# Batch 0 by whole-array products, v loaded in place, 96-row blocks, loads tied to the turns of q, part of FFN1's activation off PSUM, and the lists of the order anew

## The chip, the cores and the metric

The kernel runs on one core of one Trainium2 chip. The metric is the device time of one execution, in microseconds, as the median of the runs. Its engines each work through a queue of their own, in the order of the program: TensorE (PE) for products, VectorE (DVE), ScalarE (ACT), GpSimd (POOL), and SyncE (SP), which here only issues DMAs. GpSimd issues the loads from HBM, SyncE the DMA transposes and the stores.

## The reference

Four batches of eight heads, 768 tokens and 64 values a head, in 8 blocks of 96 tokens. A learned 8 × 8 matrix per head mixes the blocks of k and of v ("sorting"), each block of q then attends to its own sorted block, and the result goes through a two-layer network with a leaky activation.

```python
P = sort_net                                     # (4, 8, 8, 8)
for _ in range(5):                               # Sinkhorn
    P = exp(P - max(P, -1)); P = P / (sum(P, -1) + 1e-9); P = P / (sum(P, -2) + 1e-9)
k_sorted = einsum('bhij,bhjcd->bhicd', P, k_blocks)
v_sorted = einsum('bhij,bhjcd->bhicd', P, v_blocks)
scores = q_blocks @ k_sorted.T / sqrt(64)        # 96 x 96 per block and head
attn = softmax(scores); x = (attn @ v_sorted)    # -> (3072, 512), heads side by side
h = x @ w_in                                     # (512, 2048)
g = max(h, 0) + alpha * min(h, 0)
out = g @ w_out                                  # (2048, 512), float32
```

## The kernel before, in words

The work is written as operations in a graph, each with an engine (or a choice of two), a duration for the planner, the keys of what it reads and writes, and a priority. A table of numbers (`SEQ`) gives the order of all operations; a letter behind a number picks the engine where there is a choice. `arrange` lays them out by that table, and `emit` puts each engine's operations into its queue in that order, with semaphore waits only where a key asks for one. So each engine's order is fixed, and an operation that waits holds everything behind it on its engine.

The 32 blocks (four batches of eight, `g` counts them) go through `attention`, in three kinds. All of batch 0 is "near": its scores are taken, the maximum over each row found on VectorE, the scores taken again transposed and the maximum subtracted by further products (`s2`), and ScalarE's exponential gives the transposed weights directly. The later batches are "far": scores once, maximum, eight exponentials per block on ScalarE, and a DMA transpose by SyncE (`Esb` to `ET`). Then for all the output product with v, which carries a column of ones for the sum, a reciprocal and a product on VectorE (`xq`), and the transpose of `xq` into `xT`: by four products and a copy for batches 0 and 1, by a DMA transpose for batches 2 and 3.

Sorting is a product too: `prep_k` and `prep_v` multiply k or v with a small block matrix made from P (`BDK` for batch 0, `BDM` and `BDV` for the others). For the later batches k and v are first copied by GpSimd or another engine into tiles with zeros between the heads (`conv_k` into `KSz`, `conv_v` into `VDz`), so that one product uses the whole array; for batch 0, products on half the array do without for k, and v is copied into a zeroed piece of `hT`. The sorted blocks take 112 rows, 16 of them padding. q of batch 0 is loaded whole and turned by products (`prep_q`), the later batches' q is loaded per head into `QN` and turned by six DMA transposes (`turn_q`, into `QTz`).

The network runs over chunks of 2, 2, 4, 4, ... blocks. One FFN1 step (`ffn1`) is four products for 128 of the 2048 hidden columns, 192 or 384 tokens wide, into one PSUM bank; ScalarE's `Relu(-h)` and VectorE's multiply-add read that bank and write `hT`. One tile of FFN2 (`ffn2`) is 128 tokens, 16 products in four parts, all into one bank until the last part is done; most tiles use the same bank, `psY`.

All loads stand in GpSimd's queue: q, k, v of batch 0, k of batch 1, w_in in four pieces of 128 rows each, w_out in two halves, then the rest. Every FFN1 step reads all four pieces of w_in. `fill` and `idle` put products without use (`warm`, line 865) into gaps that the planner expects on TensorE up to 130 us, and a burst of 110 tiny products (line 945) starts it.

## Time and profile before

| | |
|---|---|
| median of 3 runs (lowest, highest) | 242.4 us (242.17, 244.28) |
| span of the profiled execution, first to last instruction | 240.3 us |
| TensorE busy | 231.3 us (96%), 2490 products |
| VectorE, ScalarE, GpSimd busy | 171.3, 154.1, 100.0 us |
| granted TensorE clock, mean | 1.000 |
| chain of waits: share of TensorE | 85% |

The profiled execution's own time is known by its span alone; the median of the runs lies 2.1 us above it. In the rows below, L and a number is the line of the kernel, "out<-in" names the tiles, and a time in brackets behind a row is how long the engine stood idle before it, and for whom. A product's length in a row counts until its result is written; products follow one another closer than that, so a group's length in the chain of waits, which counts from one group to the next, is its price.

### The profile page before, as it was taken

Reading aid. Unit: us, or ns where it says so; the run is one execution under the profiler, and the core shown is the slowest. Engines: PE = TensorE matmul, PEld = TensorE weight load, DVE = VectorE, ACT = ScalarE, POOL = GpSimd, SP = SyncE. Lnnn points to the kernel's source line nnn. Section 1 sums busy time; section 2 is a strip of 40 time slices with the busy share of each in tenths; the row PEclk is TensorE's granted clock in tenths of the full one; section 3 lists DMA queues with packets and bytes.
Section 4 is the critical chain, followed back from the end, with each engine's and each line's share of the span. In section 5 each row is a group of like instructions: output and inputs, shape, how many; then the busy total and the mean of one; then the engine's idle time right before and its main releaser. Section 6 shows DMA issues by size and latency. Waiting matters only on the chain.

```text
span 240.3 us, 6202 instructions
## 1 busy us (share of the span) xinstructions
PE 231.3 (96%) x2490; PEld 143.0 (59%) x2519; DVE 171.3 (71%) x347; ACT 154.1 (64%) x423; POOL 100.0 (42%) x146
## 2 busy tenths in 40 slices
...
GB/s 100 209 214 213 187 213 192 173 208 174 177 44 145 166 92 172 160 175 169 139 115 65 117 137 76 112 174 71 138 126 112 120 52 172 43 0 44 0 91 131
DMA packets 71981, 31.36 MB, mean 130 GB/s; under 512 B 64512, under 2 KB 67344, under 8 KB 71952
## 3 DMA queue, kind: packets, MB, share of 16 engines
...
q8 instruction: 20, 0.33, 0.5%
...
HBM read 27.28 MB, written 6.29 MB: 140 GB/s over the span
## 4 chain that ended last, share of the span: by engine, by line
PE 85%; POOL 5%; DMA 4%; DVE 2%; issue 1%; ACT 1%; POOLq 0%
PE psH L880 33%; PE psYP L919 29%; DMA VST<-in_v_dram 4%; PE psS L919 4%; PE psS L769 3%; PE psO L825 3%; PE psYP L726 2%; PE psYP L685 2%; POOL QN L457 2%; PE psS L784 1%; PE psYP L865 1%; POOL VDz L428 1%; PE psO L851 1%; PE psO L731 1%; PE psS L793 1%
## 5 line engine op out<-in xcount | busy, mean ns | idle before, releaser
L893 DVE SCALAR_TENSOR_TENSOR hT<-t,omaT,psH 128x384 bf16<-128x384 f32 (+1 forms) x139 | 77.8, 571 | 29.6 <-ACT t L890 27.6
L880 PE MATMUL psH<-xT,w_in_bf 128*128 128x384 bf16 (+1 forms) x556 | 98.4, 311 | 0.2 <-DVE hT L893 0.2
L890 ACT ACTIVATE t<-psH 128x384 f32<-128x384 f32 (+1 forms) x139 | 62.6, 461 | 49.8 <-PE psH L880 48.6
L919 PE MATMUL psYP<-w_out_bf,hT 128*128 128x512 bf16 x309 | 77.8, 379 | 1.7 <-DVE outstg L428 0.2
L880 PEld LDWEIGHTS psH<-xT,w_in_bf 128*128 128x128 bf16 x556 | 48.9, 98 | 28.9 <-DVE hT L893 4.1
L919 PEld LDWEIGHTS psYP<-w_out_bf,hT 128*128 128x128 bf16 x336 | 31.2, 98 | 30.3 <-DVE outstg L428 0.6
L805 ACT ACTIVATE Esb<-psS,nf 96x96 bf16<-96x96 f32 x192 | 46.2, 345 | 2.0 <-DVE nf L778 1.8
L428 POOL COPY VDz<-VST 64x384 bf16<-64x384 bf16 x40 | 34.1, 852 | 20.0 <-PE psYP L726 12.5
L672 POOL COPY KSz<-KS 64x512 bf16<-64x512 bf16 x36 | 22.6, 628 | 13.8 <-PE psYP L685 9.7
L778 DVE TENSOR_REDUCE nf<-psS 96x8 f32<-96x768 f32 x24 | 22.8, 948 | 5.5 <-PE psS L769 5.1
L836 DVE TENSOR_TENSOR xq<-psO,rec 96x512 bf16<-96x512 f32 x31 | 21.2, 684 | 0.6
L457 POOL DMA_DIRECT2D QN<-in_q_dram x24 | 19.8, 835 | 0.3 <-POOL QN L517 0.3
L865 PE MATMUL psYP<-identb 128*128 128x512 bf16 x45 | 14.8, 457 | 0.7 <-ACT identb L428 0.7
L825 PEld LDWEIGHTS psO<-VS,ET 112*128 112x128 bf16 x248 | 11.3, 98 | 4.3 <-ACT ET L816 0.2
L769 PEld LDWEIGHTS psS<-KT,QTz 128*96 128x96 bf16 x192 | 11.8, 125 | 2.5
L825 PE MATMUL psO<-VS,ET 112*128 112x65 bf16 x248 | 12.7, 194 | 0.1
L833 DVE RECIPROCAL rec<-psO 96x8 f32<-96x8 f32 x31 | 6.2, 201 | 9.1 <-PE psO L825 9.0
L428 ACT ACTIVATE VS<-psYP 112x512 bf16<-112x512 f32 x15 | 10.3, 688 | 3.6 <-PE psYP L726 3.0
L769 PE MATMUL psS<-KT,QTz 128*96 128x96 bf16 x192 | 12.6, 208 | 0.0
L428 ACT ACTIVATE KT<-psYP 128x512 bf16<-128x512 f32 x15 | 8.9, 596 | 3.9 <-PE psYP L685 2.5
L726 PE MATMUL psYP<-BDV,VDz 128*128 128x64 bf16 x192 | 9.6, 193 | 1.0 <-POOL VDz L428 0.9
L726 PEld LDWEIGHTS psYP<-BDV,VDz 128*128 128x128 bf16 x192 | 8.1, 98 | 3.9 <-POOL VDz L428 1.0
...
## 6 DMA issues: line engine op xcount, KB each, us to landing
...
KS<-in_k_dram POOLq DMA_DIRECT2D x3, 768.0 KB, 11.2
...
w_in_bf<-in_moe_w_in_dram POOLq DMA_DIRECT2D x4, 512.0 KB, 14.8
w_out_bf<-in_moe_w_out_dram POOLq DMA_DIRECT2D x2, 1024.0 KB, 22.9
...
```

The source lines that it names most:

```text
L428: return e.activation(o, i, ACTF.Copy) if e is nc.scalar else e.tensor_copy(o, i)
L457: G.add(POOL, lambda e, h=h: e.dma_start(AP(QN, h * 128 + (h // 4) * 64, [[6144, 128], [1024, 6], [1, 64]]), AP(q.tensor, b * HB + h * S * ...
L672: G.add(POOL, lambda e, hp=hp: e.tensor_copy(AP(KSz, hp * 64 * 3072 + u % 3 * 1024 + hp * 64, [[3072, 64], [128, 8], [1, 64]]), AP(KS[n], ...
L726: inst = e.matmul(AP(t, off + dd * 64, [[row, 128], [1, 64]]), AP(VDz, (u % VSL * 8 + dd) * 128, [[VSL * 1024, 128], [1, 128]]), AP(BDV, b ...
L769: inst = e.matmul(o, AP(QTz[n], hp * 3072 + h4 * 768 + i * 96, [[6144, 128], [1, 96]]), AP(KT[n], (h4 * 8 + i) * bk, [[ld, 128], [64, 2], ...
L778: G.add(DVE, lambda e: e.tensor_reduce(AP(nx, 0, [[8, 96], [4, 2], [1, 4]]), AP(psX, 0, [[1024, 96], [512, 2], [96, 4], [1, 96]]), AxisLis ...
L805: inst = e.activation(AP(Esb[me], p * 128, [[1024, 96], [64, 2], [1, 48]]), AP(psX, (p // 4) * 512 + (p % 4) * 96, [[1024, 96], [48, 2], [ ...
L825: inst = e.matmul(AP(psZ, hp * 512 + h4 * 68, [[1024, 128], [1, 65]]), AP(ET[me] if far else ET[m], pos(h4, hp) * 96, [[800, nk], [1, 128] ...
L880: inst = e.matmul(AP(pt, poff, [[1024, 128], [1, n]]), AP(w_in_bf, kt * DFF + ft * 128, [[KT_TILES * DFF, 128], [1, 128]]), AP(xT, kt * XR ...
L890: G.add(ACT, lambda e: e.activation(AP(t1[tb], 0, [[384, 128], [1, n]]), AP(pt, poff, [[1024, 128], [1, n]]), ACTF.Relu, scale=-1.0), t_ac ...
L893: G.add(DVE, lambda e: e.scalar_tensor_tensor(out=AP(hT, ft * RING + tok % RING, [[FT_TILES * RING, 128], [1, n]]), in0=AP(t1[tb], 0, [[38 ...
L919: inst = e.matmul(AP(bank[0], bank[1], [[1024, 128], [1, n]]), AP(hT, ft * RING + tok % RING, [[FT_TILES * RING, 128], [1, 128]]), AP(w_ou ...
```

## The change

- **Batch 0's sort.** k is copied into zero-spaced tiles (`KSz` and three of the `outstg` buffers) like the other batches, and sorted by whole-array products. v is loaded straight into a piece of `QTz[1]` that has been zeroed around it, in two halves, so that it needs no copy; its products take 96 columns at a stride of 64. `BDK` is gone, `spread0` makes `BDM` and `BDV` of batch 0. q of batch 0 comes in two halves by token and is turned by 48 products.
- **96-row blocks.** The padding of `KT` and `VS` to 112 rows falls away, with the copies and constants for it.
- **32-bit copies.** `conv_k` and `conv_v` move pairs of bf16 as one 32-bit element and may run on GpSimd or VectorE; the clearing of tiles may run on three engines, reading the zero tile `bz` where ScalarE does it.
- **Loads.** w_in comes in four pieces of 512 columns, each with all rows, and an FFN1 step waits for its own piece alone; w_out comes in four quarters. k and v of batch 2 are read only when all six turns of batch 1's q have landed.
- **Batch 1** turns `xq` by DMA (`TURN = 1`) instead of products.
- **FFN1's activation.** In the chunks of two blocks, five of each 16 steps (`POOLED`) have ScalarE copy the bank into `hc`, and GpSimd or VectorE forms `h - (1 - alpha) min(h, 0)` from there in two steps. The first chunk uses two banks where it used three.
- **The lists.** `SEQ` and the planner's issue times are new, so the order changes on every engine.

On GpSimd, after the first loads, before the change: w_in, then w_out's first half and v of batch 1 (`VST`), then the copies for batch 0's v (`hT`) and the first head of q (`QN`).

```order
L964 DMA w_in_bf<-in_moe_w_in_dram 128x2048
L530 MEMSET Esb 96x16x16 x2
L509 MEMSET KSz 128x1536
L964 DMA w_in_bf<-in_moe_w_in_dram 128x2048 x3
L969 DMA w_out_bf<-in_moe_w_out_dram 128x8x512
L517 MEMSET QN 128x6x64
L491 DMA VST<-in_v_dram 64x3072 x2
L428 COPY hT<-VST 128x8x48
L698 COPY KT<-KT 128x32x16
L672 COPY KSz<-KS 64x8x64
L457 DMA QN<-in_q_dram 128x6x64
```

At the same place now:

```order
L518 MEMSET QTz 64x1536
L995 DMA w_in_bf<-in_moe_w_in_dram 128x4x512 x2
L555 MEMSET Esb 96x8x16
L995 DMA w_in_bf<-in_moe_w_in_dram 128x4x512
L467 DMA QN<-in_q_dram 128x6x64
L695 COPY KSz<-KS 64x8x32 x2
L1000 DMA w_out_bf<-in_moe_w_out_dram 128x4x512
L467 DMA QN<-in_q_dram 128x6x64
L995 DMA w_in_bf<-in_moe_w_in_dram 128x4x512
L506 DMA VST<-in_v_dram 64x3072
L1010 TENSOR_SCALAR nomT<-omaT 128x16
L910 TENSOR_SCALAR t<-hc,nomT 128x192
```

The head loads of q and w_out's first quarter now stand ahead of w_in's last quarter, which follows the copies of k and a clearing of `QTz`, and v of batch 1 comes behind it; the steps of FFN1's activation (`t<-hc`) stand between the loads.

On TensorE around the first FFN1 step, with what each waits for (`d_` is a load: `wi` w_in, `wo` w_out; `s_` another engine), before:

```order
L851 MATMUL psYP<-identb,xq 128x96 x4
L851 MATMUL psO<-identb,xq 128x96 [waits s_dve]
L851 MATMUL psO<-identb,xq 128x96 x3
L613 MATMUL psYP<-Pb,selk 128x64 [waits s_act]
L613 MATMUL psYP<-Pb,selk 128x64 x2
L616 MATMUL psYP<-Pb,selk 64x64 x6
L865 MATMUL psH<-identb 128x512 x4
L880 MATMUL psH<-xT,w_in_bf 128x192 [waits d_wi0,d_wi3,d_wi2,d_wi1,s_act]
L880 MATMUL psH<-xT,w_in_bf 128x192 x3
```

and now:

```order
L864 MATMUL psO<-identb,xq 128x96 [waits s_dve]
L864 MATMUL psO<-identb,xq 128x96 x3
L878 MATMUL psH<-identb 128x512 x4
L878 MATMUL psYP<-identb 128x512
L785 MATMUL psS<-KT,QTz 96x96 [waits s_act]
L785 MATMUL psS<-KT,QTz 96x96 x7
L893 MATMUL psH<-xT,w_in_bf 128x192 [waits d_wi0,s_dve]
L893 MATMUL psH<-xT,w_in_bf 128x192 x3
L640 MATMUL psYP<-Pb,selk 128x64 [waits s_act]
L640 MATMUL psYP<-Pb,selk 128x64 x2
L643 MATMUL psYP<-Pb,selk 64x64 x6
L893 MATMUL psH<-xT,w_in_bf 128x192 x4
```

The first step waits for one piece of w_in where it waited for four.

On TensorE where the first tile of FFN2 meets w_out, before (its third part waits for the second half):

```order
L772 MATMUL psS<-KT,QTz 96x96 [waits s_act]
L772 MATMUL psS<-KT,QTz 96x96 x7
L919 MATMUL psYP<-w_out_bf,hT 128x512 [waits d_wo1]
L919 MATMUL psYP<-w_out_bf,hT 128x512 x3
L851 MATMUL psO<-identb,xq 128x96 [waits s_dve]
L851 MATMUL psO<-identb,xq 128x96 x3
```

and now, where the tile's second to fourth parts wait for a quarter each and the first score of batch 1 for the first turn of q (`d_qt0`):

```order
L945 MATMUL psYP<-w_out_bf,hT 128x512 [waits d_wo1]
L945 MATMUL psYP<-w_out_bf,hT 128x512 x3
L864 MATMUL psO<-identb,xq 128x96 [waits s_dve]
L864 MATMUL psO<-identb,xq 128x96 x3
L782 MATMUL psS<-KT,QTz 96x96 [waits d_qt0,s_act]
L782 MATMUL psS<-KT,QTz 96x96 x7
L893 MATMUL psH<-xT,w_in_bf 128x192 [waits s_dve]
L893 MATMUL psH<-xT,w_in_bf 128x192 x3
L741 MATMUL psYP<-BDV,VDz 128x64 [waits s_pool,s_act]
L741 MATMUL psYP<-BDV,VDz 128x64 x7
L893 MATMUL psH<-xT,w_in_bf 128x192 x4
L945 MATMUL psYP<-w_out_bf,hT 128x512 [waits d_wo2]
```

Behind these rows the product that waits for w_out's last quarter (`d_wo3`) comes ten rows later. Elsewhere: on VectorE the clearing of `bz`, which stood first, now follows the first Sinkhorn iteration; on SyncE `xT`'s transposes stand between `ET`'s from batch 1 on.

```diff
-BK0 = BLK + 16
...
+PHASES = [(0, 8)]
+CHUNKS = [(0, 2), (2, 4), (4, 8)]
+FAR0 = 8
+TURN = 1
+POOLED = (1, 4, 7, 10, 13)
...
 SEQ = """
-0 2 11 3 7 4 8 1 22 9 14 42 28 43 44 19 45 46 5 47 18 48 49 15 50 51 39 52 53 6 54 55 56 25 57 58 138 29 59 60
...
+27 0 5 23 22 9 13 10 36 42 43 29 44 30 11 45 46 47 48 49 50 51 41 2 1 3 14a 52 53 54 55 56 57 58 59 60 61 12a 37 39 4
...
+    def load_q0(x, prio):
+        G.add(POOL, lambda e: e.dma_start(AP(VST[0], x * 1536, [[3072, 128], [192, 8], [1, 192]]),
+                                          AP(q.tensor, x * 384 * D, [[192, 128], [S * D, 8], [1, 192]])),
+              1929, w=[("QS", x)], prio=prio, dma=(d_q[x], 0))
...
-                load_us / n, r=paced(g, x) * (b == 3), w=[(name, b % 2), (name, b % 2, x)] if x == 0 else [(name, b % 2, x)],
-                prio=prio, dma=(sem[b + x], 0))
+                load_us / n, r=paced(g, x) * (b == 3) + [("QTzt", 1, t) for t in range(6)] * (b == 2) + [("turned", 7)] * (b == 1 and FAR0 < 8), w=[(name, b % 2), (name, b % 2, x)] if x == 0 else [(name, b % 2, x)],
+                prio=prio, dma=(sem[{0: 0, 1: 1, 2: 2, 3: 6}[b] + x], 0))
...
     def load_v(b, prio):
         if b == 0:
-            load_kv(VST, v, "VST", d_v, 9, b, prio)
+            for th in range(2):
+                G.add(POOL, lambda e, th=th: e.dma_start(
+                    AP(QTz[1], th * 64 * 6144 + th * 3072, [[6144, 64], [1, 3072]]),
+                    AP(v.tensor, th * 3072, [[6144, 64], [1, 3072]])), load_us / 2,
+                    w=[("VST0", th)], prio=prio, dma=(d_v[th], 0))
             return
...
                 AP(v.tensor, b * HB + th * 3072 + c, [[6144, 64], [1, t]])), load_us / (2 * n),
-                r=[("QTzt", 0, 5)] * (b == 3), w=[("VST", b % 2)] * (x == 0) + [("VST", b % 2, x)],
-                prio=prio, dma=(d_v[2 * b - 1 + x], 0))
...
+        def f(e):
+            return copy(e, o, i) if e is nc.scalar else e.memset(o, 0.0)
+        G.add(ZERO, f, {"pool": 50 + 0.9 * n, "dve": 70 + 0.83 * n, "act": 170 + n / 1.2}, r=["bz"] + list(r), w=w, prio=prio)
...
-            for j in range(8):
-                inst = e.matmul(psYP[:, 1, 0:8], AP(sel0, j * 128, [[1024, 32], [1, 128]]),
-                                AP(Pb, j, [[64, 32], [8, 8]]), start=(j == 0), stop=(j == 7))
+            for x in range(2):
+                for j in range(8):
+                    inst = e.matmul(psYP[:, 1, x * 8:x * 8 + 8], AP(sel0, (x * 8 + j) * 128, [[2048, 32], [1, 128]]),
+                                    AP(Pb, j, [[64, 32], [8, 8]]), start=(j == 0), stop=(j == 7))
             return inst
-        G.add(PE, f, 300, r=["Pb", "sel0"], w=PSP, prio=prio)
...
+    def kslot(b, u):
+        return (outstg[u - 3], 512, 0, ("KO", u)) if b == 0 and u > 2 else (KSz, 1536, u % 3 * 512, ("KSz", u % 3))
 
     def conv_k(b, u, prio):
         n = b % 2
+        t, ld, off, key = kslot(b, u)
+        tw = KSzw if t is KSz else t
         for hp in range(2):
-            G.add(POOL, lambda e, hp=hp: e.tensor_copy(
-                AP(KSz, hp * 64 * 3072 + u % 3 * 1024 + hp * 64, [[3072, 64], [128, 8], [1, 64]]),
-                AP(KS[n], hp * 64 * 3072 + 8 * u * 64, [[3072, 64], [64, 8], [1, 64]])), 900,
-                r=[("KS", n)] + [("KS", n, x) for x in range(4)], w=[("KSz", u % 3, hp)], prio=prio)
-
...
+                kt, ld, ko, _ = kslot(b, c // 8)
+                kb = KSz if kt is KSz else outb[c // 8 - 3]
+                inst = e.matmul(AP(t, off + (c - c0) * 8 * ni, [[row, 128], [1, 8 * ni]]),
+                                AP(kb, 2 * ko + c % 8 * 128, [[2 * ld, 128], [1, 128]]),
+                                AP(BDM, b * 64 + 8 * i0, [[256, 128], [1, 8 * ni]]))
...
+            G.add(SHIFT, lambda e, o2=o2, i2=i2: e.tensor_copy(o2, i2),
+                  {"dve": 340, "pool": 519}, r=vst, w=[("VDz", u % VSL, th)], prio=prio)
...
+    def prep_v(b, d0, nd, i0, ni, prio, bank=BANK_P):
         t, off, row, keys = bank
-        n = b % 2
+        n, u = b % 2, d0 // 8
 
         def f(e):
             inst = None
-            for dd in range(8):
-                if b:
-                    inst = e.matmul(AP(t, off + dd * 64, [[row, 128], [1, 64]]),
-                                    AP(VDz, (u % VSL * 8 + dd) * 128, [[VSL * 1024, 128], [1, 128]]),
-                                    AP(BDV, b * 64, [[256, 128], [1, 64]]))
-                    continue
-                for th in range(2):
-                    inst = e.matmul(AP(t, th * 64 * row + off + dd * 64, [[row, 64], [1, 64]]),
-                                    AP(hT, (8 * u + dd) * 64, [[HR, 128], [1, 64]]),
-                                    AP(BDK, th, [[512, 128], [2, 64]]))
+            for d in range(d0, d0 + nd):
+                dd = d % 8
+                inst = e.matmul(AP(t, off + (d - d0) * 8 * ni, [[row, 128 if b else 96], [1, 8 * ni]]),
+                                AP(VDz, (u % VSL * 4 + dd // 2) * 256 + dd % 2, [[VSL * 1024, 128], [2, 128]]) if b else
+                                AP(QTz[1], d, [[6144, 128], [64, 96]]),
+                                AP(BDV, b * 64 + 8 * i0, [[256, 128], [1, 8 * ni]]))
...
-        far, me = b > 0, g % NE
-        nk = 112
+        far, me = g >= FAR0, g % NE
+        nk = 96
         pos = (lambda h4, hp: 2 * h4 + hp) if far else (lambda h4, hp: 4 * hp + h4)
...
-        if far and not (b == 1):
+        if far and b >= TURN:
             G.add(SYNC, lambda e: e.dma_start_transpose(o2, AP(xq[me], 0, [[512, 96], [1, 512]])),
                   4400 if g < 18 else 2600, r=[("xq", me)], w=[("xT", g % 16), ("turnx", g)], prio=prio, dma=(d_x[me], 0))
...
-        banks = BANK_H + ([BANK_P] if ga < 2 else [])
+        banks = BANK_H
...
-        op = G.add(PE, f, t_pe(*[(n, 128)] * 4), r=[("xT", g % 16) for g in range(ga, gb)] + [("w_in", kt) for kt in range(KT_TILES)],
+        op = G.add(PE, f, t_pe(*[(n, 128)] * 4), r=[("xT", g % 16) for g in range(ga, gb)] + [("w_in", ft // 4)],
...
+        if n == 192 and ft % 16 in POOLED:
+            y = step[0] % 2
+            h1 = AP(hc[y], 0, [[192, 128], [1, n]])
+            tt = AP(t1[tb], 0, [[384, 128], [1, n]])
+            G.add(ACT, lambda e: copy(e, h1, AP(pt, poff, [[1024, 128], [1, n]])), t_act(n), r=keys, w=[("hc", y)], prio=prio)
+            G.add(SHIFT, lambda e: e.tensor_scalar(out=tt, in0=h1, scalar1=0.0, scalar2=AP(nomT, ft, [[16, 128], [1, 1]]),
+                                                   op0=AluOpType.min, op1=AluOpType.mult),
+                  {"pool": 320, "dve": 260}, r=[("hc", y), "nomT"], w=[("t1", tb)], prio=prio)
+            G.add(SHIFT, lambda e: e.tensor_tensor(out=ho, in0=h1, in1=tt, op=AluOpType.add),
+                  {"pool": 620, "dve": 360}, r=[("hc", y), ("t1", tb)], w=hw, prio=prio)
+            return
         G.add(ACT, lambda e: e.activation(AP(t1[tb], 0, [[384, 128], [1, n]]),
...
-    load_q(0, -98)
+    load_q0(0, -98)
     load_k(0, -97)
     load_v(0, -96)
+    load_q0(1, -95.9)
     ident_op = consts()
     late_masks()
     sinkhorn()
     spread0(-48)
+    for y in range(2):
+        prep_q(0, y, -50)
     for u in range(6):
-        prep_q(u, -50, (BANK_H + BANK_O + BANK_S)[u])
-    for u in range(6):
-        prep_k(0, u, -47, BANKS0[(u + 1) % 5])
-    for u in range(8):
...
+            AP(w_in_bf, p * 512, [[KT_TILES * DFF, 128], [DFF, KT_TILES], [1, 512]]),
+            AP(moe_w_in.tensor, p * 512, [[DFF, 128], [128 * DFF, KT_TILES], [1, 512]])),
...
+            AP(w_out_bf, p * 4 * DM, [[FT_TILES * DM, 128], [DM, 4], [1, DM]]),
+            AP(moe_w_out.tensor, p * 4 * 128 * DM, [[DM, 128], [128 * DM, 4], [1, DM]])),
+            2650, w=[("w_out", p)], prio=-30 + p, dma=(dma_sem("wo%d" % p), 0))
...
-        if i == 0 and b + 1 < B:
-            if b == 0:
-                load_k(1, -26)
-            if b < 2:
-                load_q(b + 1, 8 * b - 20)
-            if b == 0:
-                load_v(1, -25)
+        if g == 8:
+            load_q(2, -12)
+        if g == 2:
+            for y in range(2):
+                prep_q(1, y, 0.9)
+            for z in PHASES[1:]:
+                phase(*z, 1, 1.5, BANK_S + BANK_O, BANK_O + [BANK_P])
         attention(g, g * 0.85 if g < 8 else g)
         if g == 1:
             spread([1, 2, 3], 1)
             G.add(PE, lambda e: warm(e, 4, (psH, 0)), 300, r=["identb"], w=[("psH", 0, 0), ("psH", 0, 1)], prio=1)
         if b + 1 < B:
-            for t in range(6 if b == 0 and i == 1 else 0):
-                turn_q(1, t, 2 + t / 2)
+            if g == 7:
+                load_k(1, -26)
```

398 lines of the change are left out of this document (200 added, 198 removed).

## The prediction

> **What bounds the kernel now.** I read the busy time by stage first, cut at the first FFN1 product (30.17), the first score product of batch 1 (58.41), 92 us and the last product (237.66). Columns: stretch, length, then busy time of each engine.
>
> ```profile
> 0.00:30.17 30.17, 26.89 (x577) 15.27 (x577) 19.24 (x66) 16.72 (x33) 24.61 (x44) 1.00 0.95 184
> 30.17:58.41 28.24, 27.74 (x424) 22.19 (x428) 24.62 (x57) 19.84 (x48) 14.96 (x22) 1.00 1.39 192
> 58.41:92.00 33.59, 32.35 (x356) 20.71 (x359) 29.49 (x56) 27.17 (x83) 26.74 (x34) 1.00 1.01 133
> 92.00:237.66 145.66, 144.33 (x1143) 84.81 (x1159) 97.91 (x170) 89.96 (x261) 33.70 (x48) 1.00 0.59 108
> ```
>
> TensorE is busy nearly throughout, but part of that is work that nobody reads: the products of line 865 only fill planned gaps. The same view for that line alone, first three stretches (the fourth has none):
>
> ```profile
> 0.00:30.17 30.17, 15.14 (x48) 4.49 (x48) 1.00 0.95 184
> 30.17:58.41 28.24, 1.52 (x5) 0.37 (x4) 1.00 1.39 192
> 58.41:92.00 33.59, 0.97 (x3) 0.29 (x3) 1.00 1.01 133
> ```
>
> So the needed work of TensorE is its busy 231.3 less 17.6 of fillers, 213.7 us. What it lost by stage (length − busy + fillers) is 18.4 in A (to 30.17), 2.0 in B (to 58.41), 2.2 in C (to 92), 1.3 in D, and 2.6 after its last product at 237.66; 213.7 + 26.6 = 240.3, the span. Only A has much to give: work moved from TensorE, or a shorter wait before FFN1, is worth its full length only if nothing later takes it back. How A begins, in order of time on TensorE:
>
> ```profile
> 1.00 1.07 PE L945 MATMUL psS<-bz 32*32 32x32 bf16 x110 [1.00 <-DVE bz L939]
> 2.79 6.29 PE L865 MATMUL psYP<-identb 128*128 128x512 bf16 x15 [0.72 <-ACT identb L428]
> 9.02 0.44 PE L656 MATMUL psS<-identb,hT 64*64 64x64 bf16 x16
> 9.29 0.67 PE L656 MATMUL psH<-identb,hT 64*64 64x64 bf16 x32
> 10.66 1.90 PE L865 MATMUL psYP<-identb 128*128 128x512 bf16 x8
> ```
>
> And how it ends (a piece of the chain of waits, then ScalarE, then TensorE; start and length):
>
> ```profile
> 5.78 10.62 DMA VST<-in_v_dram
> 28.85 0.49 ACT L428 ACTIVATE xT<-psO 128x384 bf16<-128x384 bf16 x1
> 30.17 0.49 PE L880 MATMUL psH<-xT,w_in_bf 128*128 128x192 bf16 x4
> ```
>
> q is there at 9.0, v at 16.4; the last xT copy that FFN1 wants is done at 29.34, and FFN1 starts at 30.17. The loads say why both ends meet there (issue times and times to landing of w_in and of w_out, then the first transpose that waits for q of batch 1, and the first user of k of batch 2):
>
> ```profile
> L964 POOL DMA_DIRECT2D w_in_bf<-in_moe_w_in_dram x4: 531/534/551, 8.6 to 12.2; - x4
> DMA to landing us min/median/max: 13.8/14.8/17.6
> L969 POOL DMA_DIRECT2D w_out_bf<-in_moe_w_out_dram x2: 886/905/924, 12.7 to 23.3; - x2
> DMA to landing us min/median/max: 22.7/22.9/23.1
> 51.47 12.50 SPq L465 DMA_TRANSPOSE QTz<-QN  x6
> 56.52 0.61 POOL L672 COPY KSz<-KS 64x512 bf16<-64x512 bf16 x1 [0.78 <-DMA KS<-in_k_dram]
> ```
>
> The last quarter of w_in lands at 12.2 + 17.6 = 29.8, just ahead of FFN1, and every FFN1 product needs all four quarters. One stream of loads runs without a pause: q at 9.0 and v at 16.4, with k between, is 3.7 us per 768 KB; w_in from k's next load (20.1) to 29.8 is 2.4 per quarter; w_out's first half lands at 12.7 + 22.9 = 35.6, so 2.9 per quarter; the second at 46.2; the eight head loads of q end at 51.47, 0.75 each for the seven after 46.2. A is bound by the stream and by the sorting chain of batch 0, about equally.
>
> **The change part by part.** Durations of the pieces of TensorE's work, from the chain of waits:
>
> ```profile
> 30.66 0.34 PE psS L793 x8
> 31.00 0.54 PE psS L784 x8
> 32.37 0.33 PE psYP L880 x4
> 32.70 0.31 PE psS L772 x8
> ```
>
> ```profile
> 72.33 0.36 PE psS L769 x8
> 72.69 0.17 PE psO L851 x4
> 72.86 0.86 PE psYP L919 x4
> 73.72 0.23 PE psYP L726 x8
> 73.96 0.65 PE psH L880 x4
> 74.61 0.25 PE psO L825 x8
> ```
>
> *Needed work.* Batch 1's blocks are no longer transposed on TensorE: 8 × 0.17 = 1.4 us go, and 8 DMA transposes come. Batch 0's sort becomes 48 + 64 whole-array products in place of 96 + 128 half ones, q's turn 48 in place of 96. Priced by sort products of the present kernel (0.23 per 8) or, where the stationary operand has 96 columns or 64, by score products (0.36 per 8), the three cost 4.6 to 6.5 us; today their 20 groups of 16 take about 5.5 (the second group above starts 0.27 after the first). So −0.9 to +1.0; I take 0, and 0.2 for the second spread. The 96-row blocks (112 before) leave the number of products as it is; shorter ones are worth 0 to 0.5, taken as 0. Needed: 213.7 − 1.4 + 0.2 = 212.5.
>
> *The first FFN1 product.* k now goes first and lands where q did, 9.0; half of q at 10.9, v 14.6, k of batch 1 18.3, the other half of q 20.2, a head load 20.9, and the first quarter of w_in, now all rows of 512 columns, at 23.3. FFN1's first four steps need no more than that. The chain: from v's landing to the last xT copy is 12.9 us now. The copies of v into a zero-padded tile fall away; they stand as 1.3 us ahead of the first sort product (17.7 − 16.4), and their second wave, which waits for the same engines, for perhaps 2 more. Between 12.9 − 1.3 − 2 and 12.9 − 1.3 after 14.6 is 24.2 to 26.2; I take 25.0. w_in's 23.3 is then not what ends last.
>
> One step works against this. The zero tile that TensorE's first burst reads is now cleared behind the first Sinkhorn iteration, near 4.8 us where it was 0.9, so TensorE starts about 4 us later. Above, the first 15 fillers take 6.29 us (0.42 each) and the later eight 1.90 (0.24): TensorE became fast only some 7.7 us after its first product. If it takes as long again, from 4.8, the 19 fillers now ahead of q's turn end near 13.1, when q has lain there since 10.9. The Trainium skill (TensorE: Matmul & The Clock Gate, "Part 1: The HAM clock gate") says that half rate ends after one busy window of about 3.4 us, and that the windows run freely; by that page the fillers would end, as an estimate, between 11.2 and 12.8. The trace's 7.7 us is longer than one window, as the pause between burst and fillers would make it. Either delay lies inside my 24.2 to 26.2, and does not move the sum, because a later gate decides.
>
> *Stage B.* Needed work ahead of FFN1 is 30.17 − 18.4 = 11.8 today and 11.4 with q's second half turned later, so at 25.0 TensorE has lost 13.6. From there the order on TensorE gives the work between FFN1 and each gate; up to the first product on w_out's last quarter it is 30 FFN1 steps (9.9), 6 scores (1.9), 6 second passes (5.3), 6 outputs (1.5), 5 transposes (0.9), 11 sort groups (2.5), 3 FFN2 groups (2.6) and 1.1 of small ones, 25.7 in all. ```profile
> ET<-Esb SPq DMA_TRANSPOSE x24, 2.9
> xT<-xq SPq DMA_TRANSPOSE x16, 2.4
> DMA to landing us min/median/max: 3.0/3.8/8.4
> ```
>
> (Median times to landing of the exponentials' and of xT's transposes, and below them the range of q's.) Landings, by the rates above: w_in's last quarter 34.9 (10.3 of work ahead), v of batch 1 38.6, its q 42.3, w_out's last three quarters 45.2, 48.1 and 51.0. Loss if the gate binds = landing − 11.4 − work: w_in 13.2, w_out's second 12.4 (21.4 of work), its last 13.9; the first score of batch 1 wants q's first transpose, 42.3 + 3.8 to 8.4, with 22.4 of work ahead: 12.3 to 16.9. And q's six transposes follow at 42.3, beside those three quarters. Today half of v and all of k of batch 2 stand between q's end at 51.47 and k's use at 56.52, 5.6 us of loads by the rate in 5.0 us, with the transposes running: the loads were not slowed, the transposes gave way. So w_out's gate stays near 13.9, and q's first transpose, among loads, is nearer to 8.4 than to 3.8: it lands near 49.8, with a loss of 16.0. I take that (today A and B lose 20.4). FFN2's first tile holds its PSUM bank until w_out is whole, so nothing else of FFN2 can fill in.
>
> *What costs nothing there.* In ten of the 32 narrow FFN1 steps VectorE's step off PSUM becomes a ScalarE copy and two steps on GpSimd or VectorE. FFN1 then waits for one reader of the bank, not two; hT is wanted only by FFN2, which w_out holds back. VectorE is busy 24.6 of 28.2 us in B, so this is cover for the earlier start rather than a gain. If GpSimd is late by more than the w_out gate, the lateness is paid in full (a rival).
>
> *Stage C.* GpSimd's copies of v and k and its loads of q stand in one queue today, and TensorE waited for them once:
>
> ```profile
> L428 POOL COPY VDz<-VST 64x384 bf16<-64x384 bf16 x40 | 34.1, 852 | 20.0 <-PE psYP L726 12.5 <-DMA VST<-in_v_dram 5.2
> L672 POOL COPY KSz<-KS 64x512 bf16<-64x512 bf16 x36 | 22.6, 628 | 13.8 <-PE psYP L685 9.7 <-DMA KS<-in_k_dram 2.6 <-POOL VDz L428 0.2
> 83.52 0.41 PE L726 MATMUL psYP<-BDV,VDz 128*128 128x64 bf16 x8 [0.87 <-POOL VDz L428]
> ```
>
> These copies now move pairs of elements as 32-bit words: half as many. By element that is 0.43 and 0.31 us, by byte 0.85 and 0.63. The 0.87 wait and most of the 1.0 of fillers go; new waits for batch 1's xT come. 2.2 becomes 1.5, bounds 0.5 and 3.
>
> *Sum.* 212.5 + 16.0 + 1.5 + 1.3 + 2.6 = 233.9 us of span against 240.3. The median of the runs, 242.4, is 2.1 above the profiled span, and I carry that over: 236.0.
>
> **The rivals.** *The loads decide (no change).* The transposes and w_out share the engines evenly while both are queued. Six transposes took 12.5 us today; in that time w_out would get half, 6.25 of its 8.7, so its last quarter lands at 42.3 + 12.5 + 2.45 = 57.3, the loss is 20.2, the span 238.1 and the time 240.2. The Trainium skill (DMA: Bandwidth & Descriptors, "Queues, rings and completion order") says each DMA engine takes turns between the queues that have work, packet by packet, which speaks for this one; the 5.0 us above speak against it.
>
> *GpSimd paces stage B (no change).* From 25.5 to 39 it has 8 copies of k, 6 loads of q, 4 other loads and 4 pairs of FFN1 steps. A pair priced by its copies above, 1.2 to 2.2 ns an element and two operands in the second, is 0.7 to 1.3 us: 12.6 to 18 us in 13.5. Up to 5 late gives 238.9, or 241.0.
>
> *Batch 1 turns twice (slower).* Each of its blocks now goes through two DMA transposes, in the stretch where k, v and q of batch 2 are all loaded, since these loads now wait for batch 1's q.
>
> Its steps, as groups:
>
> ```profile
> L805 ACT ACTIVATE Esb<-psS,nf 96x96 bf16<-96x96 f32 x192 | 46.2, 345 | 2.0 <-DVE nf L778 1.8
> L778 DVE TENSOR_REDUCE nf<-psS 96x8 f32<-96x768 f32 x24 | 22.8, 948 | 5.5 <-PE psS L769 5.1
> L836 DVE TENSOR_TENSOR xq<-psO,rec 96x512 bf16<-96x512 f32 x31 | 21.2, 684 | 0.6
> ```
>
> A block's chain is score 0.36, maximum 0.95, exponentials 46.2/24 = 1.9, turn 2.9, output 0.25, product 0.68, turn 2.4: 4.15 + 5.3. Three buffers make that 3.2 us per block, while TensorE has 4 FFN1 groups (2.6), 3 FFN2 groups (2.6), 0.6 of attention and 0.4 of sort, 6.2. It decides from (3 × 6.2 − 4.15)/2 = 7.2 us a turn. q's longest turn, beside loads, took 8.4. At 9.5 the block takes 7.7, 1.5 more for 8 blocks: 12 us, a span of 245.9, a time of 248.0. Against it: xT's median of 2.4, and later batches already turn twice.
>
> *The gates do not bind (better).* Loss 13.6, stage C at 0.5, sort at −0.9: 229.6, or 231.7.
>
> **How the numbers follow.** Forecast 0.60 (233 to 239.5); better 0.10; loads decide 0.10; GpSimd 0.08; twice turned 0.12. About 1% (2.4 us) is what a measurement here can tell from no change. Faster by more than that is forecast plus better, 0.70; the two that land within it 0.18; slower 0.12. The high end of the unknown costs, sort +1.0, w_out 20.2, stage C 3, gives 240.6 + 2.1 = 242.7; with GpSimd a little late, 243.5. The range 231.5 to 243.5 leaves out the slower case and a sliver on each side.
>
> **What would show it.** Right: the first FFN1 product between 24 and 26.5; no fillers after it; the first product on w_out's last quarter at 50 to 55, and TensorE waiting for a load or a transpose of q just ahead of it; 29 fillers in all; from 92 us on the same loss as now. Wrong: FFN1 later than 27 (then the sorting chain or the cold start was mispriced); long waits of TensorE for hT from GpSimd in B; FFN1 of blocks 8 to 11 waiting for a DMA transpose; transposes of batch 1 longer than 7 us.

## The result, and the profile after

The changed kernel takes 259.6 us (median of four runs, 257.5 to 261.9) against 242.9 for the kernel before on the same chip: a ratio of 1.0645, 95% interval 1.0555 to 1.0735. It is slower by 16.7 us, where 6.4 us faster was forecast. Times here and below are medians of all runs of a kernel, ratios come from its runs within 1.5% of the fastest, and since the profiles of the runs called E1, E7, E9, E15 and E17 below were slower than that, only landmarks and single rows of those are used. The profiled execution has a span of 258.9 us; TensorE is busy for 233.8 us, at a mean granted clock of 0.954 where it was 1.000.

The same stages as in the prediction, cut at the landmarks of the changed kernel: first FFN1 product (34.47), first score product of batch 1 (60.81), 92 us, end of the last product (256.2). Stretch, length, busy time of TensorE, weight loads, VectorE, ScalarE and GpSimd, then the granted clock, the DMA share and GB/s:

```profile
0.00:34.47 34.47, 29.14 (x385) 22.59 (x385) 18.34 (x66) 18.77 (x32) 20.10 (x37) 0.80 1.17 184
34.47:60.81 26.34, 23.19 (x404) 19.06 (x402) 20.86 (x48) 17.18 (x42) 23.67 (x37) 1.00 1.14 137
60.81:92.00 31.19, 22.20 (x218) 14.04 (x218) 17.09 (x36) 16.22 (x53) 18.03 (x31) 0.84 1.09 106
92.00:256.20 164.20, 159.24 (x1292) 94.05 (x1310) 111.85 (x200) 100.50 (x291) 31.34 (x58) 1.00 0.70 114
```

All 29 fillers lie in the first stretch. The same view for their line alone:

```profile
0.00:34.47 34.47, 8.62 (x29) 2.89 (x29) 0.80 1.17 184
```

So the ledger of the prediction, made again: needed work 233.8 − 8.6 = 225.2 us, lost in A 5.3 + 8.6 = 14.0, in B 3.1, in C 9.0, in D 5.0, behind the last product 2.7. Against the forecast (212.5; A and B together 16.0; 1.5; 1.3; 2.6) the needed work is 12.7 over, A and B 1.1, C 7.5, D 3.7. Two places stand out: needed work, and stage C.

The first place is the sort of batch 0's v. Rows of TensorE's timeline from there to FFN1, most of them of line 741, the sort (start, length, engine, line, operation, output<-inputs):

```profile
15.22 2.79 PE L741 MATMUL psO<-BDV,QTz 128*96 128x64 bf16 x16
17.84 1.50 PE L741 MATMUL psYP<-BDV,QTz 128*96 128x64 bf16 x8
19.75 2.82 PE L741 MATMUL psO<-BDV,QTz 128*96 128x64 bf16 x16
25.96 1.52 PE L741 MATMUL psO<-BDV,QTz 128*96 128x64 bf16 x8
34.47 0.50 PE L893 MATMUL psH<-xT,w_in_bf 128*128 128x192 bf16 x4
```

The second group starts 2.62 us after the first, which has 16 products: 0.164 us each. The weight loads of 48 of the 64 products (minimum, median and maximum in ns, then first and last start) take the time:

```profile
L741 PEld LDWEIGHTS psO<-BDV,QTz x48: 237/257/258, 15.2 to 27.1; 128*96 128x96 bf16 x48
```

And from about 18 us on the clock is at half, though by the profile TensorE is busy throughout (length, busy time of TensorE, weight loads and the other engines, clock, DMA):

```profile
16.00:18.00 2.00, 2.00 (x14) 2.00 (x14) 0.81 (x2) 0.27 (x1) 1.96 (x4) 1.00 1.23 179
20.00:22.00 2.00, 2.00 (x14) 2.00 (x13) 1.23 (x3) 0.69 (x1) 2.00 (x4) 0.50 1.27 209
```

Busy counts a product until its result is written. The page's row of the granted clock, in 40 slices of 6.5 us, shows this spell and a second one near 80 to 90 us:

```profile
PEclk9995599999996599999999999999999999999999
```

The second spell follows the second place. A piece of the chain of waits (start, length, what): the exponentials of block 9, the second of batch 1, are done at 69.7, and their transpose lands 14.25 us later.

```profile
68.44 1.27 ACT Esb L818 x5
69.71 0.03 ACT t L916
69.74 14.25 DMA ET<-Esb
83.99 0.14 issue
84.13 0.60 PE psO L838 x8
```

What TensorE waited for over the whole span (us in total, times, longest), and what was issued to the DMA engines from 70 to 75 us, with the median time to landing:

```profile
PE psO L838 <- DMA ET<-Esb: 11.5, 4, 7.8
PE psS L971 <- DVE bz L965: 5.0, 1, 5.0
```

```profile
KS<-in_k_dram POOLq DMA_DIRECT2D x4, 192.0 KB, 12.5
VST<-in_v_dram POOLq DMA_DIRECT2D x2, 192.0 KB, 10.0
QN<-in_q_dram POOLq DMA_DIRECT2D x2, 96.0 KB, 14.3
ET<-Esb SPq DMA_TRANSPOSE x1, 14.3
```

The times to landing of all transposes of exponentials (minimum, median, maximum), before and after:

```profile
DMA to landing us min/median/max: 2.8/2.9/5.3
DMA to landing us min/median/max: 2.8/3.1/14.3
```

Batch 2's k and v, which now wait for batch 1's q, and its q are loaded just where batch 1's blocks need their transposes. Before, TensorE's list of waits has none for a transpose of exponentials.

### The profile page after: what moved, and what is told of

It reads as the page before. It is cut to its first block, busy times and chain, and to the rows that moved or that the text cites. A ratio compares the mean times of both kernels' runs of the same rounds, so it can differ in the third digit from the quotient of the medians.

```text
span 258.9 us, 5845 instructions
## 1 busy us (share of the span) xinstructions
PE 233.8 (90%) x2282; PEld 149.7 (58%) x2309; DVE 168.1 (65%) x348; ACT 153.1 (59%) x418; POOL 93.1 (36%) x162
## 4 chain that ended last, share of the span: by engine, by line
PE 69%; DMA 17%; POOL 8%; issue 2%; ACT 2%; DVE 1%; POOLq 0%; ACTq 0%
PE psH L893 26%; PE psYP L945 23%; DMA ET<-Esb 13%; DMA VST<-in_q_dram 4%; PE psS L945 3%; PE psO L741 3%; PE psS L782 3%; PE psYP L741 3%; PE psO L838 2%; POOL t L910 2%; POOL VDz L730 1%; POOL hT L913 1%; POOL KSz L695 1%; PE psYP L709 1%; POOL QN L467 1%
## 5 line engine op out<-in xcount | busy, mean ns | idle before, releaser
L893 PE MATMUL psH<-xT,w_in_bf 128*128 128x384 bf16 (+1 forms) x576 | 101.7, 311 | 0.7 <-ACT hc L437 0.7
L945 PE MATMUL psYP<-w_out_bf,hT 128*128 128x512 bf16 x309 | 79.9, 381 | 1.7 <-issue 0.4
L893 PEld LDWEIGHTS psH<-xT,w_in_bf 128*128 128x128 bf16 x576 | 51.4, 98 | 31.0 <-DVE hT L919 2.4
L945 PEld LDWEIGHTS psYP<-w_out_bf,hT 128*128 128x128 bf16 x336 | 31.3, 98 | 28.9 <-issue 0.7
L730 POOL COPY VDz<-VST 64x192 f32<-64x192 f32 x40 | 21.1, 527 | 23.5 <-DMA VST<-in_v_dram 15.6
L838 PE MATMUL psO<-VS,ET 96*128 96x65 bf16 x248 | 13.1, 197 | 11.5 <-DMA ET<-Esb 11.5
L695 POOL COPY KSz<-KS 64x256 f32<-64x256 f32 x34 | 13.9, 409 | 24.6 <-PE psYP L709 22.6
L838 PEld LDWEIGHTS psO<-VS,ET 96*128 96x128 bf16 x248 | 11.4, 99 | 16.5 <-DVE hT L919 9.3
L437 ACT ACTIVATE VS<-psYP 96x512 bf16<-96x512 f32 x16 | 10.9, 681 | 11.7 <-PE psYP L741 11.6
L910 POOL TENSOR_SCALAR t<-hc,nomT 128x192 f32<-128x192 f32 x8 | 7.5, 932 | 9.5 <-ACT hc L437 8.8
L437 DVE CAST VS<-psYP 96x512 bf16<-96x512 f32 x10 | 6.9, 689 | 5.6 <-PE psYP L741 5.6
## 6 DMA issues: line engine op xcount, KB each, us to landing
w_in_bf<-in_moe_w_in_dram POOLq DMA_DIRECT2D x4, 512.0 KB, 11.7
```

The lines of the kernel that those rows point to most:

```text
L730: G.add(SHIFT, lambda e, o2=o2, i2=i2: e.tensor_copy(o2, i2), {"dve": 340, "pool": 519}, r=vst, w=[("VDz", u % VSL, th)], prio=prio)
L838: inst = e.matmul(AP(psZ, hp * 512 + h4 * 68, [[1024, 128], [1, 65]]), AP(ET[me] if far else ET[m], pos(h4, hp) * 96, [[800, nk], [1, 128] ...
L893: inst = e.matmul(AP(pt, poff, [[1024, 128], [1, n]]), AP(w_in_bf, kt * DFF + ft * 128, [[KT_TILES * DFF, 128], [1, 128]]), AP(xT, kt * XR ...
L945: inst = e.matmul(AP(bank[0], bank[1], [[1024, 128], [1, n]]), AP(hT, ft * RING + tok % RING, [[FT_TILES * RING, 128], [1, 128]]), AP(w_ou ...
```

## The experiments

The theory after the first look had two causes: the stationary operand of the v products, whose columns lie 64 elements apart (S), and batch 2's loads beside the transposes (C). Rivals were the GpSimd steps of FFN1 and their effect on the loads queued behind them, the second DMA turn of batch 1's blocks, and loads that set the pace whatever is mended.

Landmarks of the profiled runs, in us: first FFN1 product; VectorE's row maximum (line 791, one per block) of block 8, the first of batch 1, and of block 12; span. Where an expectation says "first score product of batch 2" or "of batch 2's first", the stretch that it quotes for the changed kernels (26.5 and so on) runs to block 12, the fifth block of batch 1; it is so read here. The kernel before was run beside each set of experiments and has medians from 242.4 to 244.3 us there, so across sets the ratios compare better than the times.

| kernel | FFN1 | block 8 | block 12 | span | median of the runs (lowest to highest) |
|---|---|---|---|---|---|
| before | 30.2 | 59.1 | 78.6 | 240.3 | 242.9 |
| after | 34.5 | 61.4 | 92.6 | 258.9 | 259.6 (257.5 to 261.9) |
| E1 adjacent columns | 26.7 | 56.2 | 83.5 | 253.7 | 254.8 (249.2 to 256.9) |
| E2 no GpSimd steps | 36.0 | 66.8 | 91.7 | 259.2 | 262.6 (261.2 to 263.3) |
| E3 small loads, batch 2 | 37.0 | 63.8 | 84.3 | 250.9 | 251.6 (250.4 to 252.6) |
| E4 v copied first | 31.4 | 58.2 | 84.7 | 251.5 | 253.5 (253.1 to 258.1) |
| E5 = E1 + E3 | 26.5 | 53.3 | 77.4 | 245.4 | 247.7 (246.2 to 249.7) |
| E6 loads early, v first | 30.6 | 68.5 | 87.6 | 255.2 | 257.5 (256.9 to 260.3) |
| E7 xT by TensorE | 35.8 | 62.6 | 93.2 | 264.8 | 264.6 (262.5 to 266.5) |
| E9 loads early, q first | 31.8 | 66.3 | 86.0 | 255.2 | 255.1 (252.3 to 257.9) |
| E10 before + 8 loads | 30.3 | 59.4 | 82.0 | 244.4 | 248.0 (246.1 to 249.2) |
| E11 = E5, batch 3 too | 26.7 | 55.9 | 76.4 | 239.5 | 240.1 (238.4 to 244.4) |
| E12 = E9, start repaired | 30.1 | 65.0 | 84.6 | 252.5 | 253.1 (252.7 to 254.3) |
| E13 runs of 128 | 31.3 | 58.1 | 80.7 | 253.3 | 253.5 (251.7 to 255.1) |
| E14 runs of 256 | 31.4 | 58.3 | 82.2 | 250.2 | 252.0 (251.9 to 253.2) |
| E15 = E13, start repaired | 29.8 | 56.6 | 79.1 | 253.3 | 255.3 (250.4 to 257.5) |
| E16 loads early, turns last | 29.5 | 63.6 | 82.8 | 252.7 | 254.3 (252.8 to 254.6) |
| E17 = E16, few fillers | 34.0 | 62.1 | 81.3 | 253.8 | 252.1 (250.8 to 255.6) |

**E1: adjacent columns.** The same products in number and size, which read other elements of v.

```diff
-   AP(QTz[1], d, [[6144, 128], [64, 96]]),
+   AP(QTz[1], d * 96, [[6144, 128], [1, 96]]),
```

> Left out: batch 0's v is not sorted rightly (the 64 sort products read 96 adjacent columns of the loaded v instead of every 64th; same products, same order, same copies). Theory S (the stationary operand with a step of 64 columns costs the time): one such product falls from 0.17 to 0.19 us to 0.03 to 0.05, the 64 of them from about 11 us to 2 to 3; the granted clock no longer falls to half between 18 and 33 us; the first FFN1 product moves from 34.47 to between 22 and 26; the time falls from about 259.6 to 247 to 254, more if the loads behind the GpSimd steps move up with FFN1, less if w_out and q of batch 1 decide stage B. Rival L (the loads and GpSimd's queue pace the first 60 us whatever the sort takes): first FFN1 earlier, but the first score product of batch 1 stays within 2 us of 60.8 and the time at 257 or more.

The weight loads of line 741 and the first FFN1 product in this run:

```profile
L741 PEld LDWEIGHTS psO<-BDV,QTz x48: 119/125/125, 16.6 to 20.5; 128*96 128x96 bf16 x48
26.66 0.50 PE L893 MATMUL psH<-xT,w_in_bf 128*128 128x192 bf16 x4
```

The 64 products now take 4.2 us from first to last (16.61 to 20.78) where they took 12.3, the clock stays full up to FFN1, and FFN1 starts 7.8 us earlier. S is right about the start. The time gives only about 5 of it back (median; the four runs spread over 7.7 us, and from fastest to fastest run it is 8.3). Block 8 already comes only 5.2 us earlier, as TensorE now waits 2.6 us for a turn of batch 1's q. Stage C keeps its wait: from block 8 to block 12 it is 27.3 us here, 31.2 in the changed kernel, 19.5 before.

**E8: the step alone, measured.** Behind the last products of the kernel before, groups of products that nobody reads, each group with another step between the 96 stationary columns.

```diff
+    G.add(PE, lambda e: [e.matmul(lo[d % 8], AP(QTz[1], d % 16, [[6144, 128], [64, 96]]), lm) for d in range(16)][-1], 500, **lad)
```

(and one such line for each other step, which stands where this one has 64)

> The kernel before, with products that nobody reads behind its last ones: groups of 16 products of 96 columns of a tile against 64 columns, with steps between the stationary columns of 1, 2, 4, 8, 16, 32, 62 and 64 elements, then 32 with a step of 1, 64 with a step of 64, and 32 with a step of 1. If the cost grows with the distance: a weight load under 0.1 us at steps 1 and 2, growing to 0.25 at 64, and 62 as 64. If it is a conflict of powers of two: 62 takes as little as 1. Clock: the granted clock falls to half some us into the 64 products with a step of 64 if TensorE's sparse use is what lowers it, and stays full if the late start of the changed kernel was. Time about 20 us above the kernel before.

TensorE's timeline there; lines 1046 to 1053 are the steps 1, 2, 4, 8, 16, 32, 62 and 64, the next one 32 products with step 1:

```profile
240.09 0.87 PE L1046 MATMUL psH<-BDV,QTz 128*96 128x64 bf16 x16
240.80 0.91 PE L1047 MATMUL psH<-BDV,QTz 128*96 128x64 bf16 x16
241.55 1.61 PE L1048 MATMUL psH<-BDV,QTz 128*96 128x64 bf16 x16
242.99 2.98 PE L1049 MATMUL psH<-BDV,QTz 128*96 128x64 bf16 x16
245.81 3.06 PE L1050 MATMUL psH<-BDV,QTz 128*96 128x64 bf16 x16
248.69 2.80 PE L1051 MATMUL psH<-BDV,QTz 128*96 128x64 bf16 x16
251.30 2.96 PE L1052 MATMUL psH<-BDV,QTz 128*96 128x64 bf16 x16
254.07 2.80 PE L1053 MATMUL psH<-BDV,QTz 128*96 128x64 bf16 x16
256.69 2.75 PE L1054 MATMUL psH<-BDV,QTz 128*96 128x64 bf16 x32
259.25 10.62 PE L1055 MATMUL psH<-BDV,QTz 128*96 128x64 bf16 x64
```

From start to start, per product: 44 ns at step 1, 47 at 2, 90 at 4, 176 at 8, 180 at 16, 163 at 32, 173 at 62, 164 at 64. The clock had fallen by the step of 32; at full clock the step of 64 took the same 164 ns in the changed kernel. It is neither the distance beyond 8 elements nor a power of two. Windows over the same place (length, TensorE's busy time, weight loads, the other engines, clock):

```profile
244.00:246.00 2.00, 2.00 (x14) 2.00 (x13) 0.00 (x0) 0.00 (x0) 0.00 (x0) 1.00 0.00 0
248.00:250.00 2.00, 2.00 (x14) 2.00 (x14) 0.00 (x0) 0.00 (x0) 0.00 (x0) 0.50 0.05 8
```

The clock falls to half some 3 to 5 us after the slow weight loads begin, with TensorE busy 2.00 of 2.00 us by the profile on both sides. The adjacent columns at 256.7 then take 80 ns each, the step of 64 the same 163 as at full clock. So here TensorE lost its clock without a gap in the profile, while it mostly loaded weights, and it is the work behind that pays. The Trainium skill (SBUF — State Buffer, the note on 16-byte lines in "Door 1: The DMA port swizzle") has the cause that fits: SBUF is read in lines of 16 bytes, and each access to a new line costs. Its figure, a step of 8 elements of bf16 for free, is not what these rows show: two are free, four cost twice, eight four times. That it is flat from 8 elements on, which are 16 bytes, fits such lines; no run here tests the cause apart.

**E4: a copy that removes the step, nothing left out.** Eight VectorE copies lay v out in pairs, so that the step is 2, as it is for the later batches.

```diff
+   for u in range(8):
+       G.add(SHIFT, lambda e, u=u: e.tensor_copy(AP(hTw, 4 * u * 96, [[FT_TILES * RING // 2, 128], [1, 96], [96, 4]]),
+                                                 AP(QTw, 4 * u, [[3072, 128], [32, 96], [1, 4]])),
...
-   AP(QTz[1], d, [[6144, 128], [64, 96]]),
+   AP(hT, (d // 2) * 192 + d % 2, [[FT_TILES * RING, 128], [2, 96]]),
```

> Nothing left out: eight VectorE copies turn the loaded v of batch 0 into pairs of tokens' columns, so that the 64 sort products read a stationary operand with a step of 2 columns, as those of the later batches do. Theory S: the products take 0.03 to 0.05 us each, the copies 0.4 to 0.6 us each, so that the sort of v takes 4 to 5.5 us instead of 12; first FFN1 product at 24 to 28; time 249 to 255, within 2 us of the run that reads adjacent columns. Rival: VectorE, which also takes a part of the copies off PSUM there, makes it slower, first FFN1 after 30, time above 256.

253.5 us, 6.1 below the changed kernel (ratio to before 1.0437, 1.0406 to 1.0467). FFN1 starts at 31.4, later than expected: the copies, 0.36 us each, stand together ahead of VectorE's copies off PSUM, TensorE waits 1.4 us for those, until 19.3, is busy for 0.62 us from 18 to 20, and the clock still drops to half there. So this run prices the step only together with its remedy.

**E2: no GpSimd steps in FFN1.**

```diff
-POOLED = (1, 4, 7, 10, 13)
+POOLED = ()
```

> The ten narrow FFN1 steps that went over GpSimd get ScalarE's and VectorE's step straight from PSUM again; all else as in the changed kernel. Theory G (GpSimd's steps of 0.93 and 0.6 us, and the loads that stand behind them in its queue, held stage B): w_out's last quarter is issued at 45 to 50 instead of 56.3, the first score product of batch 1 comes at 54 to 58 instead of 60.8, and the time falls by 3 to 6 us, to 254 to 257. Rival V (VectorE takes the work over and paces instead, or the late start alone decides): between 258 and 262.

262.6 us (ratio 1.0809, 1.0768 to 1.0849), slower than the changed kernel with 1.0645. GpSimd issues w_out's last quarter here at

```profile
55.52 0.74 POOL L999 DMA_DIRECT2D w_out_bf<-in_moe_w_out_dram  x1
```

so hardly earlier than the changed kernel's 56.3: other copies in the queue, which wait for TensorE, hold it. The time is above what both theories gave, and G's gain doesn't come. But the plan also puts 25 fillers (6.7 us) into stage B here, where the changed kernel has none, so that the 3 us aren't shown to be what the steps are worth, and G is not tested cleanly.

**E3: small loads for batch 2.** Most of k's and v's elements are not fetched.

```diff
-   AP(src.tensor, b * HB + x * 3072 // n, [[3072, 128], [1, 3072 // n]])),
+   AP(src.tensor, b * HB + x * 3072 // n, [[3072, 128], [1, 96 if b == 2 else 3072 // n]])),
```

(and the like for the destination and for v)

> Left out: of k and v of batch 2 only an eighth (a sixteenth of v's columns per piece stays in shape, 96 columns of each piece) is loaded; the same eight issues at the same places. Theory C (in 70 to 85 us the exponentials' transposes wait for the DMA engines, which batch 2's loads fill): the longest time to landing of such a transpose falls from 14.3 to 5 us or less, TensorE's gap at 75.5 to 84 closes to 2 us or less, the clock stays full there, and the time falls by 8 to 12 us, to 248 to 252. Rival Q (the transposes are late because they stand behind one another and the exponentials behind ScalarE's other work): the gap stays above 5 us and the time above 256.

```profile
PE psO L838 <- DMA ET<-Esb: 2.4, 2, 2.2
```

251.6 us, 8.0 below (ratio 1.0360, 1.0321 to 1.0399). The gap at 75 is gone, block 8 to block 12 takes 20.5 us instead of 31.2, and the waits for transposes are 2.4 us instead of 11.5. The longest transpose from 60 to 100 us takes 4.5 us; one after 100 us still takes 8.9, where it holds TensorE less. Theory C holds in its main point.

**E7: one turn per block.**

```diff
-TURN = 1
+TURN = 2
```

> Nothing left out. The changed kernel with batch 1's blocks transposed for xT by TensorE again (eight groups of four products and eight copies), so that its blocks go through one DMA transpose each, as before the change. If the second DMA turn costs what the rival of the forecast said: time down by 8 us or more, to below 252. Theory C (it is the loads of batch 2 that hold the exponentials' transposes, whatever xT does): 257 to 262, and the wait for the exponentials' transposes near 75 us stays over 5 us.

```profile
PE psO L838 <- DMA ET<-Esb: 8.9, 2, 7.4
```

264.6 us: slower, by some 5, not faster by 8, and above C's 257 to 262; the plan has 28 more fillers after 62 us here. The wait near 75 us is still 7.4. The second turn is not what holds batch 1.

**E10: the same loads added to the kernel before.**

```diff
+    for x in range(8):
+        t, src, real = ((KS[1], k, (647, 650)), (VST[1], v, (643, 646)))[x // 4]
+        c = x % 4 * 768
+        op = G.add(POOL, lambda e, t=t, src=src, c=c: e.dma_start(
+            AP(t, c, [[3072, 128], [1, 768]]), AP(src.tensor, 2 * HB + c, [[3072, 128], [1, 768]])),
...
```

(192 KB each, into the buffers of k and v of batch 1; GpSimd issues them from 64.5 us on)

> The kernel before, with eight further loads of 192 KB that nobody reads (into the buffers of k and v of batch 1 once these are done with), issued by GpSimd at about 64 us, where the changed kernel issues k and v of batch 2. Theory C: the transposes of exponentials between 64 and 82 take 8 to 14 us to landing instead of at most 5.3, TensorE waits 4 to 9 us for them, and the time rises to 247 to 253. Rival (a transpose beside loads is not slower here, or the three buffers hide it): at most 2 us, up to 245, and that from the 4.4 us that the issues take of GpSimd.

A piece of the chain of waits of this run:

```profile
66.04 11.73 DMA ET<-Esb
```

The longest transpose of exponentials is 11.7 us where it was 5.3; the time is 248.0, a ratio of 1.021 (1.014 to 1.029). Block 8 to block 12 takes 22.6 us instead of 19.5. So loads beside a transpose slow it in a kernel that has nothing else of the change. What that costs isn't shown: TensorE waits only 0.5 us for transposes, not the 4 to 9 expected, with 18 fillers from 59 to 82 us where the kernel before has one, and the eight issues also hold GpSimd for 4.3 us, behind which its copies come later. The 4.5 us lost may be due to either.

**E5 and E11: both causes away, then batch 3's loads as well.** E5 has the edits of E1 and E3. E11 has the condition `b > 1` where E5 has `b == 2`.

> Left out: batch 0's v is sorted from adjacent columns, and of k and v of batch 2 only 96 columns of each piece are loaded; both edits of the two runs before in one kernel. If the two costs (the step of the stationary operand, and batch 2's loads beside the transposes) are separate and are all that the change costs: about 259.6 - 5 - 8 = 246 to 247, range 243 to 249, the first FFN1 product near 26.7 and no wait of TensorE for a transposed tile over 2.5 us. Rival (the collision is one of the consequences of the late start, or something third costs as much): 250 or more; or, if the half clock cost on top of both, below 242.

> As the run with both edits (247.7): left out is the right sorting of batch 0's v and most of k and v of batch 2, and here of k and v of batch 3 too (96 columns of each piece). If what is still lost in the stages of batches 2 and 3 (3.0 and 2.1 us idle on TensorE, waits for the transposes of exponentials) is the same collision with batch 3's loads: 242 to 244.5, and no idle stretch over 1 us between 100 and 155. Rival (those waits are the transposes of q, xT and the exponentials among themselves): 246.5 or more.

E5: 247.7, about as expected from adding the two (ratio 1.017, 1.006 to 1.028). E11: 240.1, a ratio of 0.985 (0.977 to 0.993), below the expected 242 to 244.5 and 1.5% below the kernel before. With the step, batch 2's loads and batch 3's loads away, no loss is left. E11 is no kernel that one could use: it also spares the DMA engines bytes that the kernel before has to load, so that it doesn't show what the rest of the change is worth. How much of the 7.6 us between E5 and E11 is collision, and how much the bytes alone, it doesn't tell.

With the start near the forecast, E11 also shows the gate of stage B (TensorE, with its wait):

```profile
55.18 0.64 PE L782 MATMUL psS<-KT,QTz 128*96 128x96 bf16 x8 [2.05 <-DMA QTz<-QN]
```

**E6 and E9: the same loads, earlier.** On E4, the loads of batch 2 wait for no turn of q, and GpSimd issues them ahead of its first FFN1 step. The edit for v (the line's end is left out), and the like for k:

```diff
-               r=[("QTzt", 0, 5)] * (b == 3) + [("QTzt", 1, t) for t in range(6)] * (b == 2) + [("turned", 7)] * (b == 1 and FAR0 < 8),
+               r=[("QTzt", 0, 5)] * (b == 3) + [("turned", 7)] * (b == 1 and FAR0 < 8),
```

> Nothing left out. Beside the VectorE copies of v (253.5): the second half of v of batch 1, the last five loads of its q, three quarters of w_out and k of batch 2 are issued one behind another in GpSimd's queue ahead of the first GpSimd step of FFN1, and v of batch 2 as soon as q's last turn has left its buffer; the loads of batch 2 wait for no turn of q any more. Theory C (the late loads, tied to q's turns and held in GpSimd's queue, then lie beside the transposes of the exponentials): w_out's last quarter is issued before 35 instead of 53, all loads of k and v of batch 2 have landed by about 62, the longest transpose of exponentials takes 6 us or less instead of 10.2, and the time falls by 6 to 9 us to 244 to 248. Rival R (queued earlier they slow the turns of q of batch 1, so that the first score product of batch 1 comes at 60 or later): 251 to 256.

> Nothing left out; the earlier run with early loads had v of batch 2 by mistake ahead of the rest in GpSimd's queue, where it waited 9.7 us for q's last turn. Here the second half of v of batch 1, q of batch 1, w_out, k of batch 2 and then v of batch 2 are issued in this order right behind the first half of v of batch 1, ahead of the first GpSimd step of FFN1 (with the VectorE copies of v of batch 0 as in the 253.5 run). Theory C: all loads of batch 2 have landed by 64, the first score product of batch 1 comes at 57 to 61, the stretch from there to the first of batch 2 takes 19 to 21 us instead of 26.5, and the time is 245 to 249. Rival R (the loads only change places: the turns of q of batch 1 now lie beside them): first score product of batch 1 at 62 or later, time 251 or more.

In E6 v of batch 2 stands ahead of everything else in the queue, and GpSimd waits 9.7 us there: 257.5, which says nothing on C. E9 has v last. Times to landing of q's turns (minimum, median, maximum) in E9:

```profile
DMA to landing us min/median/max: 3.0/4.3/20.7
```

Block 8 to block 12 takes 19.7 us, as C says, but block 8 comes at 66.3, as R says; 255.1 us (ratio 1.039). In batch 1 the loads moved the collision from the exponentials' transposes to q's.

**E13 and E14: the same bytes in smaller packets.** On E4; k's and v's loads of batches 2 and 3 in runs of 128 or 256 elements.

```diff
-                AP(t[b % 2], x * 3072 // n, [[3072, 128], [1, 3072 // n]]),
+                AP(t[b % 2], x * 128, [[3072, 128], [512, 6], [1, 128]]) if b > 1 else AP(t[b % 2], 0, [[3072, 128], [1, 3072]]),
```

(and the like for the source and for v)

> Nothing left out. The run with the VectorE copies of v of batch 0 (253.5), with the loads of k and v of batches 2 and 3 cut into runs of 128 elements (512 B read) instead of 768 and 1536 (3 and 6 KB), the same bytes in the same number of loads issued at the same places. Theory P (the DMA engines take turns packet by packet, so a transpose's small packets wait behind the loads' large ones): the longest transpose of exponentials falls from 10.2 to 7 us or less, the stretch from the first score product of batch 1 to that of batch 2 from 26.5 to 20 to 23, and the time to 245 to 250. Rival B (the bytes decide, and smaller packets only make the loads slower): longest transpose 10 us or more, time 253 or more.

> As the run beside it, with runs of 256 elements (1 KB read). Theory P: between the two, longest transpose 7 to 9 us, time 247 to 252. Rival B: 253 or more.

Block 8 to block 12 takes 22.6 us with runs of 128 and 24.0 with 256, against 26.5 in E4, and the longest transpose 8.5 and 9.1 us against 10.2 (one profile each): shorter runs help the transposes. That fits the Trainium skill (DMA: Bandwidth & Descriptors, "Queues, rings and completion order": each engine takes turns between queues packet by packet). What was won is lost again: from block 12 to the end the two take 172.6 and 168.0 us against 166.8, and GpSimd waits 8.7 and 7.9 us for v of batch 3 where it waited 7.2. The times, 253.5 and 252.0, lie within the spread of E4. Neither theory comes out whole: with runs of 128 the time is the rival's and the transpose between the two, with 256 the time is at the end of P's range.

**E12, E15, E16, E17: repairs.** E12 is E9, and E15 is E13, with each copy of v three groups ahead of its products and ten fillers among them. In E12 a planned filler overwrote one sort product's bank before it was read, so its batch 0 is not the reference's; the work is the same.

> Nothing left out. As the run with the early loads in the right order, and the eight copies of v of batch 0 stand three groups ahead of their products instead of all in front, with ten filler products of TensorE among the first groups so that it isn't idle there. Theory: sort of v ends at 21 to 22.5 instead of 24.1, the clock stays full there, first FFN1 product at 26.5 to 29 and the time 2 to 4 us under the run beside it if the start still counts, 0 to 1 us if the loads gate stage B anyway (theory C's and R's common ground).

> Nothing left out. Runs of 128 elements as in the first of these three, and the copies of v of batch 0 three groups ahead of their products with ten fillers among them; no planned filler falls on a bank of a sort product that is not yet read, as one did in the earlier run of this arrangement, whose batch 0 was therefore wrong. If the start counts: first FFN1 product at 26.5 to 30 instead of 31.4 and 1 to 4 us below the first of these three, 242 to 248; if stage B's loads swallow it: within 1 us of it.

FFN1 starts at 30.1 and 29.8 at full clock, 1.7 and 1.5 us earlier than in E9 and E13. E12 takes 253.1, E15 255.3 (250.4 to 257.5): no gain from the earlier start is seen in the time. E16 issues w_out and k of batch 2 ahead of the last five loads of batch 1's q, and E17 caps its planned fillers at four in a gap.

> Nothing left out. The repaired start (copies of v of batch 0 ahead of their products with ten fillers among them), the loads in runs as in the changed kernel, and the loads of w_out and of k of batch 2 issued ahead of the last five loads of q of batch 1, v of batch 2 behind them: q lands late, but its turns then lie beside 0.8 MB of loads instead of 3.1. If what counts is that turns and loads do not lie side by side: first score product of batch 1 at 57 to 61 instead of 65.7 in the run with q first, no turn of q over 10 us, the stretch from it to the first score product of batch 2 at 19 to 21 us, time 245 to 249. If the sum of the DMA work alone decides, whatever the order: first score product of batch 1 at 64 or later and the time at 252 or more.

> Nothing left out. The run with the turns last had its first turn of q landed at 58.1, but the plan had put 32 filler products (6.9 us) ahead of the first score product of batch 1, which came at 63.0. Here at most four fillers stand in one planned gap. If the order of loads and turns is what counts: first score product of batch 1 at 57.5 to 60, the stretch to batch 2's first still 19 to 20, time 248.5 to 251. If the fillers only stood where TensorE would have waited: 62 or later, and 253 to 255.

In E16 q's turns take at most 7.2 us, and the first lands at 58.1; but the chain of waits shows fillers ahead of block 8:

```profile
56.25 6.92 PE psH L881 x32
```

E17 has block 8 at 62.1 in a profile whose start was at half clock, and 252.1 us (ratio 1.034, 1.028 to 1.040), against 254.3 (1.045, 1.038 to 1.053) for E16. The order helps the turns; that it alone recovers the time isn't shown. No repaired version has a median under 252 us, and none beats the kernel before.

## Why the prediction was wrong, point by point

*The needed work, 212.5.* This is the first step that failed. The three sorts of batch 0 were "taken 0", between −0.9 and +1.0, with the 96-column stationary operands priced "by score products (0.36 per 8)". The score products read adjacent columns. The v products have a step of 64 in the diff's own access pattern, no product of the kernel before has a step above 2, and so no row could price it; this bound was too narrow. Measured: 1.3 us per 8, 10.9 us in all (the pieces on the chain) instead of 2.9, so +8.0. With both causes away TensorE's busy time less fillers is 222.9 − 8.1 = 214.8 (E5) and 223.9 − 9.6 = 214.3 (E11): the remaining terms of this step were right to some 2 us. The last 2.5 or so of the 12.7 go with the two causes; other products at half clock, behind the sort and behind the gap of stage C, fit them, but were not priced one by one.

*The first FFN1 product at 25.0 (24.2 to 26.2).* 34.5; with adjacent columns 26.5 to 26.7 (E1, E5, E11), still 0.3 to 0.5 above the range. The chain was nearly right: v, which the sum had at 14.6, landed at 14.9 in the changed kernel and at 16.7 in E11. The late zero tile cost nothing, as said: the fillers end at 11.4 and q's turn starts at 11.6, when q is there. My own 13.1 was too late; the row below agrees with the 11.2 to 12.8 worked out there from the rule of the Trainium skill (TensorE: Matmul & The Clock Gate, "Part 1: The HAM clock gate"). TensorE's timeline at the fillers:

```profile
6.03 5.35 PE L878 MATMUL psYP<-identb 128*128 128x512 bf16 x19
```

*Loss of A and B, 16.0.* Measured 17.1. The size was right by luck: w_out's last quarter, forecast to land at 51.0, was not issued until 56.3, and TensorE, itself late, waited neither for it nor for a turn of q in B. Where the start is near the forecast, A and B lose 18.3 (E5) and 20.4 us (E11). The gate that the sum took, the turn of q ahead of batch 1's first score, binds in E1 and E11. There q is loaded by 43.6 and 43.7, near the 42.3 of the sum, but the turn lands at 55.5 and 55.1, not 49.8: beside w_out's loads turns took up to 10.6 and 9.1 us. This term was 2 to 4 us too small.

*What costs nothing in B.* GpSimd's pair takes 0.93 + 0.59 = 1.5 us, above the 0.7 to 1.3:

```profile
L910 POOL TENSOR_SCALAR t<-hc,nomT x8: 927/929/946, 35.4 to 66.1; 128x192 f32<-128x192 f32 x8
L913 POOL TENSOR_TENSOR hT<-hc,t x8: 590/592/625, 37.4 to 67.1; 128x192 bf16<-128x192 f32 x8
```

In B TensorE waits once, 0.7 us, for ScalarE's copy, 1.6 us in all for GpSimd's copies of v, and never for hT. So the steps are mostly cover, as said, and the rival's up to 5 us don't show, though the chain of waits runs along GpSimd's queue for most of 35 to 59 us. That they would hold back the loads behind them in the queue was not seen; E2, with its fillers, doesn't settle what that cost.

*Stage C, 1.5 (0.5 to 3).* 9.0 measured, and the range did not hold it. The failed step is that only GpSimd's copies were costed there. The loads of batch 2, moved into this stage by the tie to q's turns, were costed on their own queue and not on SP's. The rival "batch 1 turns twice" had the place and named those loads, at 12 us from a turn of 9.5 where 7.5 came; but its mechanism, the second turn, is not it (E7): a single transpose of 14 us beside loads makes the wait, which goes with the loads (E3). The sentence that misled is "the loads were not slowed, the transposes gave way": it was used against the case where the loads decide and not carried on to the transposes that would have to give way.

*Stage D, 1.3, and the tail, 2.6.* 5.0 and 2.7. In D 3.8 us are waits for transposes of exponentials; with batch 3's loads small too, E11 is another 7.6 us below E5.

*The rivals.* Slower had 0.12, by one mechanism; the two that came together were the collision behind that rival and a price that no rival carried. The range up to 243.5 missed by 16 us. Two of the signs of being wrong came: FFN1 later than 27, and transposes of batch 1 longer than 7 us.
